# Where the softmax divides in the first sixteen pairs: on the output of a block of tokens, with the first two weight conversions done the older way

## The chip, the core and the metric

The kernel runs on one core of a Trainium2 chip. The metric is the device time of one execution in microseconds: 673.12 us, the median of three runs (672.76 to 674.39). Five things work side by side: TensorE (PE, matmuls, results into PSUM), VectorE (DVE), ScalarE (ACT), GpSimd (POOL, nearly unused here), and SyncE (SP), which issues the loads. Each has a queue of its own, worked off in the order in which the program wrote it; they meet through semaphores.

## What is computed

An attention with a window and four sink tokens, followed by two MLPs, on 2 x 768 tokens:

```
scores = q k^T / 8           2 batches, 8 heads, 768 tokens, head size 64
keep   = key < 4 (sinks)  or  0 <= query - key < 128
a      = exp(scores - max);   a = a / (sum(a) + 1e-9)
x      = a v                  -> 1536 tokens x 512
g      = max(h,0) + alpha*min(h,0),  h = x w_in      2048 wide
y      = g w_out
z      = (h2 - tanh(h2)) w_out2,     h2 = y w_in2
```

The weights come in as 64-bit floats and are turned into fp32 on the chip.

## The kernel before

Tokens are worked in twelve *blocks* `u` of 128, each in four *pairs* of heads: pair `n` = 4u + p, 48 in all. For a pair TensorE makes the scores of its two heads (`s_mm`, six matmuls, since queries and keys are split into a high and a low half), 288 columns wide: the block's own keys, the block's before, 32 sink keys. Block 0 has 128. VectorE adds the mask and takes the maximum (`s_max`, L279), ScalarE makes the exponentials with their row sums in the same instruction (`s_exp`, L288). VectorE adds 1e-9 to the sums and inverts them (`norm_sum`, L294, L296: "factors" below) and multiplies the two heads' rows by them (`norm`, L303). Only then does TensorE transpose the rows (`t_mm`, L319), alternating between the PSUM tiles `t` and `h`; ScalarE evicts them (`t_ev`, L326); TensorE multiplies them with the values (`pv`, L358, L359). From the third block of a batch on, the sink columns of two pairs are copied together (`sink_copy`, L309), transposed (`sink_mm`), evicted (`sink_ev`) and multiplied in (`pv`, L362). When a block's four pairs are there, its output in PSUM is split into a high half (`x_h`, ScalarE, L369) and a low half (`x_l`, VectorE, L374): the input of the first MLP.

The first 19 rounds `n` (S_LEAD) are attention alone, here called the lead. Round n makes the scores of pair n+1, maxima and exponentials of pair n, normalisation and transposes of pair n-1, outputs of pair n-2; a block's `x_h` stands at the end of the round after its last pair's transposes (n % 4 == 1), its `x_l` one round later. In between stand the splits of a key group for later pairs (`kq_hi` on ScalarE, L234, `kq_lo` on VectorE, L237; every other round) and two weight conversions, begun in rounds 8 and 12 and worked off one VectorE step a round. Of a conversion (`convert_scaled`) ScalarE does two steps (L73, L74), VectorE two (L76, L78), each 1024 columns wide. In round 14 the first weight is split for its matmuls (`split_w`, ScalarE, L215; `split_lo`, VectorE, L220).

After the lead the steps `g` of the MLPs begin (`h_mm`, `out_mm`), 96 in all, and the remaining pairs run among them, one a step (L678 to L801). The order is written out by hand: each engine gets its instructions in the order in which these lines call it, and the tiles' pools add the waits for a buffer to come free.

Of the kernel before, what the change touches and what calls it, by code (L numbers as in the profile page):

```python
# [9 lines left out]
F32 = mybir.dt.float32  # L10
# [5 lines left out]
AF = mybir.ActivationFunctionType  # L16
ALU = mybir.AluOpType
# [3 lines left out]


S_LEAD = 19
CONV0 = ((0, 8), (1, 12))
B, H, S, D = 2, 8, 768, 64
NB = S // 128
# [16 lines left out]
W_UP, W_DOWN = 2.0 ** -111, 2.0 ** -8  # L43
# [24 lines left out]
def convert_scaled(nc, pair, dst, seen):  # L68

    lw, hw = pair[:, :, 0], pair[:, :, 1]  # L70
    top = pair.bitcast(U16)[:, :, 1]
    di = dst.bitcast(I32)
    nc.scalar.activation(out=dst, in_=hw.bitcast(F32), func=AF.Abs, scale=W_UP, accum_out=seen)  # L73
    nc.scalar.activation(out=lw, in_=top, func=AF.Copy, scale=1.0 / 8192, bias=FLOOR)  # L74
    yield
    nc.vector.scalar_tensor_tensor(di, di, 3, lw, op0=ALU.logical_shift_left, op1=ALU.bitwise_or)  # L76
    yield
    nc.vector.scalar_tensor_tensor(di, hw, SIGN, di, op0=ALU.bitwise_and, op1=ALU.bitwise_or)  # L78
# [60 lines left out]
def fast_path(tc, qk, v, vsink, limits, w1i, w1o, alpha, w2i, w2o, out, outer):  # L139
    nc = tc.nc  # L140
    keep = outer.enter_context(tc.tile_pool(name="keep", bufs=1))
    bad_i = keep.tile([1, 1], I32, name="bad_i")
    with ExitStack() as ctx:
# [56 lines left out]
        def conv_w(m, f):  # L200
            raw = stage[m][f % 2]
            if m == 1 and f < 3:
                wf[m, f] = ap.tile([128, 1024], F32, name="wf", tag="wx" if f == 2 else "pq", bufs=1 if f == 2 else 2)
            else:
                wf[m, f] = wp.tile([128, 1024], F32, name="wf", tag="wf", bufs=NF)
            at = m * NF + f
            yield from convert_scaled(nc, raw.rearrange("p (n t) -> p n t", t=2), wf[m, f], seen[:, at:at + 1])

        whl = {}

        def split_w(m, c, f, part):
            src = wf[m, f][:, 512 * part:512 * part + 512]
            hi = wp.tile([128, 512], F32R, name=f"wh{part}", tag=f"wh{part}", bufs=2)
            lo = wp.tile([128, 512], F32R, name=f"wl{part}", tag=f"wl{part}", bufs=2)
            nc.scalar.activation(out=hi, in_=src, func=AF.Copy, scale=W_DOWN)  # L215
            whl[m, c, f, part] = (hi, lo)

        def split_lo(m, c, f, part):
            hi, lo = whl[m, c, f, part]
            nc.vector.scalar_tensor_tensor(lo, wf[m, f][:, 512 * part:512 * part + 512], W_DOWN, hi, op0=ALU.mult, op1=ALU.subtract)  # L220


        x_t, y_t = {}, {}
        pq, sums, ptb, pts, vps, sks, sps, tps = {}, {}, {}, {}, {}, {}, {}, {}
        initial = [True]
        rot = [0]

# [17 lines left out]
        def ps_tile(tags):  # L245
            rot[0] += 1
            tag = tags[rot[0] % len(tags)]
            return ps.tile([128, 512], F32, name="ps_" + tag, tag=tag, bufs=4 if tag == "o" else 1)
# [23 lines left out]
        def s_max(n, a):  # L272
            u, p, b, i, w = geom(n)
            G, hh = 2 * u + p // 2, 2 * (p % 2) + a
            if hh == 0:
                pq[G] = ap.tile([128, 4, 288], F32, name="pq", bufs=2)
                sums[G] = ap.tile([128, 4], F32, name="sums", bufs=2)
            mask = m_zero if i == 0 else m_one if i == 1 else m_even if i % 2 == 0 else m_odd
            nc.vector.tensor_tensor_reduce(  # L279
                out=pq[G][:, hh, 0:w], in0=sps.pop((n, a))[:, :w], in1=mask[:, 0:w], scale=-0.125, scalar=BIG,  # L280
                op0=ALU.add, op1=ALU.min, accum_out=nm[:, 2 * n + a:2 * n + a + 1],
            )

        def s_exp(n, a):
            u, p, b, i, w = geom(n)
            G, hh = 2 * u + p // 2, 2 * (p % 2) + a
            e = pq[G][:, hh, 0:w]
            nc.scalar.activation(out=e, in_=e, func=AF.Exp, scale=-1.0, bias=nm[:, 2 * n + a:2 * n + a + 1], accum_out=sums[G][:, hh:hh + 1])  # L288

        def norm_sum(n, part):  # L290
            u, p, b, i, w = geom(n)
            r = sums[2 * u + p // 2][:, 2 * (p % 2):2 * (p % 2) + 2]
            if part == 0:
                nc.vector.tensor_scalar(r, r, 1e-9, None, op0=ALU.add)  # L294
            else:
                nc.vector.reciprocal(r, r)  # L296

        def norm(n):
            u, p, b, i, w = geom(n)
            G, hh = 2 * u + p // 2, 2 * (p % 2)  # L300
            for a in range(2):
                e = pq[G][:, hh + a, 0:w]
                nc.vector.tensor_scalar(e, e, sums[G][:, hh + a:hh + a + 1], None, op0=ALU.mult)  # L303
        def sink_copy(n):
            u, p, b, i, w = geom(n)
            G = 2 * u + p // 2
# [4 lines left out]
        def t_mm(n):  # L311
            u, p, b, i, w = geom(n)
            G, hh = 2 * u + p // 2, 2 * (p % 2)
            tps[n] = t = ps_tile(["t", "h"] if initial[0] else ["t"])
            cur = 0 if i % 2 == 0 else 160
            for a in range(2):
                for e, c in ((0, 160 - cur), (1, cur)):
                    if i > 0 or e == 1:
                        nc.tensor.transpose(t[:, 256 * a + 128 * e:256 * a + 128 * e + 128], pq[G][:, hh + a, c:c + 128], ident)  # L319

        def t_ev(n):
            u, p, b, i, w = geom(n)
            ptb[n] = ap.tile([128, 2, 2, 128], F32, name="pt", bufs=2)
            e0 = 1 if i == 0 else 0
            tv = tps.pop(n).rearrange("p (a e c) -> p a e c", a=2, e=2)
            nc.scalar.activation(out=ptb[n][:, :, e0:, :], in_=tv[:, :, e0:, :], func=AF.Copy)  # L326
# [5 lines left out]
        def sink_mm(n, share):  # L332

            G = n // 2
            tag = ["o"] if initial[0] else ["s"]
            a = 1 if initial[0] else 0
            s = sps[share, a] if (share, a) in sps else ps_tile(tag)
            if share < NPAIR:
                sps[share, a] = s
            tps[n, 0] = s  # L340
            nc.tensor.transpose(s[:, 384:512], sks.pop(G).rearrange("p h c -> p (h c)"), ident)
# [22 lines left out]
        def x_h(n):  # L364
            u = n // 4
            c, off = divmod(u * 128, CH)
            if off == 0:
                x_t[c] = xp.tile([128, 2, 4, CH], F32R, name="x", tag="x")
            nc.scalar.activation(out=x_t[c][:, 0, :, off:off + 128], in_=vps[u], func=AF.Copy)  # L369

        def x_l(n):
            u = n // 4
            c, off = divmod(u * 128, CH)
            nc.vector.tensor_tensor(x_t[c][:, 1, :, off:off + 128], vps.pop(u), x_t[c][:, 0, :, off:off + 128], op=ALU.subtract)  # L374


        h_ps, gt, o_ps, mid, ob = {}, {}, {}, {}, {}
# [92 lines left out]
        nc.vector.memset(warm, 0.0)  # L470
        nc.vector.memset(shift, SQ_C)
        nc.vector.memset(limit, -POLY_T2)
        nc.vector.memset(m_one[:, 128:160], -BIG)
        nc.scalar.activation(out=warm, in_=warm, func=AF.Exp)
        load_qk(0)
# [79 lines left out]

        for n in range(S_LEAD):
            last = n == S_LEAD - 1
            a_loads(n)
            if n == 0:
                s_mm(0)  # L560
            if not last:
                s_mm(n + 1)
            if n >= 2:
                t_ev(n - 2)
            s_max(n, 0)
            s_max(n, 1)
            s_exp(n, 0)
            s_exp(n, 1)
            if n >= 2 and has_sinks(n - 2):
                sink_ev(n - 2)  # L570
            if n >= 1:
                norm_sum(n - 1, 0)
                norm_sum(n - 1, 1)
                norm(n - 1)
                sink_copy(n - 1)
                if not last:
                    t_mm(n - 1)
                    if has_sinks(n - 1):
                        sink_mm(n - 1, n + 1)
            if n >= 2 and not last:  # L580
                pv(n - 2)
            splits_hi(n)
            if n >= 5 and n % 4 == 1:
                x_h(n - 2)
            splits_lo(n)
            if n >= 5 and n % 4 == 2:
                x_l(n - 3)
            if n == 1:
                masks(0)
            if n == 4:  # L590
                masks(1)
            if n == 3:
                load_w(0, 1)
            for f, at in CONV0:
                if n == at:
                    conv_start(0, f)
                if at < n < at + 5:
                    conv_step(0, f)
                if n == at + 4:
                    load_w(0, f + 2)  # L600
                if n == at + 6 and f == 0:
                    split_w(0, 0, 0, 0)
                    split_lo(0, 0, 0, 0)
# [378 lines left out]
```

## Time and profile before

| | |
|---|---|
| median of 3 runs | 673.12 us |
| the profiled execution: its own time, its span | 672.06 us, 670.3 us |
| PE busy | 636.5 us, 95% |
| DVE busy | 526.3 us, 79% |
| ACT busy | 471.9 us, 70% |
| chain that ended last | PE 80%, DVE 8%, ACT 7% |

The page cuts the span into 40 slices of 16.8 us and gives busy shares in tenths (9 is 90% or more) and the clock granted to TensorE:

```profile
PE   4967999999999999999899999999999999999995
...
DVE  5887989899576665558877777889998888888873
ACT  4886988787566564557766767877877777777763
...
PEclk9997899999999999999999999999999999999999
```

A time line prints instructions in order of time: start, duration, engine, line, operation, tiles. Neighbours of one kind are merged (x4). A bracket says how long the engine had been idle before, and what ended the wait. VectorE and ScalarE overlap the end of one instruction with the start of the next, so a step (from start to start) is a little shorter than a duration.

### The profile page before, as it was taken

The page shows a single profiled execution, that of the slowest core. Times are in us where ns is not written, and L with a number is a line of the kernel's source. Part 1 is how long each engine was busy: PE and PEld are TensorE (multiplying, and loading weights), DVE is VectorE, ACT ScalarE, POOL GpSimd, SP SyncE. Part 2 cuts the span into 40 slices and gives each one's busy share as a digit, 9 for nine tenths or more (in the row PEclk, how much of TensorE's full clock was granted, in tenths as well). Part 3 has the DMA queues.
Part 4 walks back from the last instruction along what each step waited for, and adds up shares of the span by engine and source line. Part 5 has one row for each costly group of instructions (what it writes and reads, how often), then busy time and mean ns, then how long its engine had stood idle before and what let it go on. Part 6 is the DMA issues. An engine that isn't in the chain of part 4 may idle for free.

```text
span 670.3 us, 9201 instructions
## 1 busy us (share of the span) xinstructions
PE 636.5 (95%) x3194; PEld 501.2 (75%) x3194; DVE 526.3 (79%) x1098; ACT 471.9 (70%) x936; POOL 1.1 (0%) x8
## 2 busy tenths in 40 slices
PE   4967999999999999999899999999999999999995
PEld 2545677777777777777788887887888888888884
DVE  5887989899576665558877777889998888888873
ACT  4886988787566564557766767877877777777763
POOL 0000000000000000000000000000000000000000
PEclk9997899999999999999999999999999999999999
DMA  4752344453010000204343420100010000100001
GB/s 110 220 160 94 142 157 165 164 206 111 10 39 17 1 16 1 103 25 152 119 169 127 163 89 1 63 1 0 1 63 1 2 0 1 63 1 1 0 1 68
DMA packets 27032, 47.36 MB, mean 71 GB/s; under 512 B 3168, under 2 KB 15456, under 8 KB 26976
## 3 DMA queue, kind: packets, MB, share of 16 engines
q1 hardware_dynamic: 26976, 46.68, 20.3%
q8 instruction: 27, 0.44, 0.3%
q14 instruction: 29, 0.24, 0.1%
HBM read 43.53 MB, written 3.15 MB: 70 GB/s over the span
## 4 chain that ended last, share of the span: by engine, by line
PE 80%; DVE 8%; ACT 7%; issue 2%; SPq 1%; DMA 1%; ACTq 0%; DVEq 0%
PE ps_o L441 34%; PE ps_h L389 22%; PE ps_s L389 7%; PE ps_t L389 6%; PE ps_t L319 2%; PE ps_s L270 2%; PE ps_v L358 2%; PE ps_v L359 2%; PE ps_v L362 2%; ACT raw L74 1%; ACT wf L73 1%; PE ps_o L270 1%; DVE wf L78 1%; SPq L180 1%; DVE pq L279 1%
## 5 line engine op out<-in xcount | busy, mean ns | idle before, releaser
L220 DVE SCALAR_TENSOR_TENSOR wl<-wf,wh 128x512 fp32r<-128x512 f32 x192 | 123.6, 685 | 45.2 <-ACT wh L215 45.2
L389 PE MATMUL ps_h<-x,wh 128*128 128x512 f32 x384 | 124.5, 405 | 2.2 <-ACT t L396 1.9
L215 ACT ACTIVATE wh<-wf 128x512 fp32r<-128x512 f32 x192 | 111.0, 630 | 5.2 <-PE ps_o L441 5.2
L389 PEld LDWEIGHTS ps_h<-x,wh 128*128 128x128 f32 x384 | 68.7, 189 | 18.1 <-ACT t L396 3.1
L441 PE MATMUL ps_o<-gh,wh 128*128 128x512 f32 x192 | 76.6, 399 | 0.3 <-DVE y L452 0.3
L389 PE MATMUL ps_h<-x,wl 128*128 128x512 f32 x192 | 75.5, 393 | 0.0
L441 PE MATMUL ps_o<-wh,gh 128*128 128x512 f32 x192 | 74.8, 390 | 0.2 <-ACT gh L420 0.2
L441 PE MATMUL ps_o<-gh,wl 128*128 128x512 f32 x192 | 74.9, 390 | 0.0
L441 PE MATMUL ps_o<-gl,wh 128*128 128x512 f32 x192 | 74.8, 390 | 0.0
L441 PE MATMUL ps_o<-wh,gl 128*128 128x512 f32 x192 | 74.8, 390 | 0.0
L441 PE MATMUL ps_o<-wl,gh 128*128 128x512 f32 x192 | 74.7, 389 | 0.0
L288 ACT ACTIVATE pq<-pq,nm 128x288 f32<-128x288 f32 (+1 forms) x96 | 48.4, 506 | 28.6 <-DVE nm L279 28.2
L420 ACT ACTIVATE gh<-g 128x512 fp32r<-128x512 f32 x48 | 30.4, 633 | 36.4 <-DVE g L127 36.4
L76 DVE SCALAR_TENSOR_TENSOR wf<-wf,raw 128x1024 int32<-128x1024 int32 x32 | 39.1, 1222 | 18.7 <-ACT raw L74 18.6
L326 ACT ACTIVATE pt<-ps_t 128x512 f32<-128x512 f32 (+1 forms) x39 | 21.8, 560 | 35.5 <-PE ps_t L319 35.5
L441 PEld LDWEIGHTS ps_o<-gh,wh 128*128 128x128 f32 x192 | 36.1, 188 | 9.1 <-issue 1.4
L420 ACT ACTIVATE gh<-t 128x512 fp32r<-128x512 f32 x48 | 30.1, 627 | 18.1 <-DVE t L408 18.1
L389 PEld LDWEIGHTS ps_h<-x,wl 128*128 128x128 f32 x192 | 36.2, 188 | 8.0
L441 PEld LDWEIGHTS ps_o<-wh,gh 128*128 128x128 f32 x192 | 36.0, 188 | 8.1 <-ACT gh L420 0.6
L441 PEld LDWEIGHTS ps_o<-wh,gl 128*128 128x128 f32 x192 | 36.0, 188 | 7.9 <-DVE gl L425 0.4
L441 PEld LDWEIGHTS ps_o<-gh,wl 128*128 128x128 f32 x192 | 36.0, 188 | 7.8
L441 PEld LDWEIGHTS ps_o<-wl,gh 128*128 128x128 f32 x192 | 36.0, 188 | 7.5
(145 smaller groups left out, 1285.2 us busy)
## 6 DMA issues: line engine op xcount, KB each, us to landing
raw<-in_moe_w_in_dram SPq DMA_DIRECT2D x32, 512.0 KB, 3.3
raw<-in_moe_w_out_dram SPq DMA_DIRECT2D x32, 512.0 KB, 4.3
raw_qk<-in_qk_dram SPq DMA_DIRECT2D x96, 64.0 KB, 2.9
vt<-in_v_dram SPq DMA_DIRECT2D x12, 256.0 KB, 2.8
out_dram<-ob SPq DMA_DIRECT2D x2, 1024.0 KB, 4.2
out_dram<-ob SPq DMA_DIRECT2D x4, 256.0 KB, 3.4
vs<-in_vsink_dram SPq DMA_DIRECT2D x2, 256.0 KB, 3.6
ns_raw<-in_limits_dram SPq DMA_DIRECT2D x1, 2.0 KB, 2.6
```

What stands on the lines that cost most here:

```text
L76: nc.vector.scalar_tensor_tensor(di, di, 3, lw, op0=ALU.logical_shift_left, op1=ALU.bitwise_or)
L215: nc.scalar.activation(out=hi, in_=src, func=AF.Copy, scale=W_DOWN)
L220: nc.vector.scalar_tensor_tensor(lo, wf[m, f][:, 512 * part:512 * part + 512], W_DOWN, hi, op0=ALU.mult, op1=ALU.subtract)
L270: nc.tensor.matmul(sps[n, a][:, :w], lhsT=kq[l][h, p, at:at + 128], rhs=kq[r][h, p, K_EVEN:K_EVEN + w], start=e == 0, stop=e == 2)
L288: nc.scalar.activation(out=e, in_=e, func=AF.Exp, scale=-1.0, bias=nm[:, 2 * n + a:2 * n + a + 1], accum_out=sums[G][:, hh:hh + 1])
L319: nc.tensor.transpose(t[:, 256 * a + 128 * e:256 * a + 128 * e + 128], pq[G][:, hh + a, c:c + 128], ident)
L326: nc.scalar.activation(out=ptb[n][:, :, e0:, :], in_=tv[:, :, e0:, :], func=AF.Copy)
L358: nc.tensor.matmul(d, lhsT=vt[u - 1][:, h * D:(h + 1) * D], rhs=pt[:, a, 0, :], start=p == 0, stop=False)
L359: nc.tensor.matmul(d, lhsT=vt[u][:, h * D:(h + 1) * D], rhs=pt[:, a, 1, :], start=p == 0 and i == 0, stop=p == 3 and i < 2)
L389: nc.tensor.matmul(h_ps[f], lhsT=l[:, w], rhs=x[:, r, kk, :], start=kk == 0 and e == 0, stop=kk == 3 and e == 2)
L420: nc.scalar.activation(out=gh, in_=mid[f], func=AF.Copy)
L441: nc.tensor.matmul(o, lhsT=l, rhs=r, start=f == 0 and e == 0, stop=f == NF - 1 and e == 2)
```

## The change

For the pairs of the first four blocks (`u < LATE`) the rows are no longer normalised before they are transposed. Their sums lie in one tile of eight columns a block; after the fourth pair all eight are inverted at once. TensorE then spreads the factors: `late_mm` multiplies, head by head, a column of factors broadcast to 64 columns with the identity, so that a PSUM tile `ps_r` holds the factor of every token in every row of the block's output (eight matmuls). `late_copy` copies it to SBUF, `late_norm` multiplies the block's output in PSUM by it, and `x_h` and `x_l` read the product. `ps_r` lies where the second transpose tile lay, so in the lead the transposes have one tile in place of two. `x_h` moves from the end of round n % 4 == 1 into the next round, behind that round's exponentials and key split (in the last round it is issued earlier). Pairs 16 on are normalised as before.

The first two conversions use `convert_weights`: on ScalarE one step without a sum, on VectorE four. Their check against a limit goes away (`seen` is cleared at the start), and their weights need no scale.

```diff
+LATE = 4
...
@@ conv_w
+            if m == 0 and f < len(CONV0):
+                yield from convert_weights(nc, raw.rearrange("p (n t) -> p n t", t=2), wf[m, f])
+                return
             yield from convert_scaled(nc, raw.rearrange("p (n t) -> p n t", t=2), wf[m, f], seen[:, at:at + 1])
...
+        def down(m, f):
+            return 1.0 if m == 0 and f < len(CONV0) else W_DOWN
-            nc.scalar.activation(out=hi, in_=src, func=AF.Copy, scale=W_DOWN)
+            nc.scalar.activation(out=hi, in_=src, func=AF.Copy, scale=down(m, f))
...
@@ s_max, s_exp
-                sums[G] = ap.tile([128, 4], F32, name="sums", bufs=2)
+                if p == 0:
+                    sums[u] = ap.tile([128, 8], F32, name="sums", bufs=2)
...
@@ norm_sum
+            if u < LATE and p < 3:
+                return
+            r = sums[u] if u < LATE else sums[u][:, 2 * p:2 * p + 2]
...
@@ norm
+            if u < LATE:
+                return
...
+        def late_mm(n):
+            u = n // 4
+            rps[u] = ps.tile([128, 4, 128], F32, name="ps_r", tag="h", bufs=1)
+            for h in range(8):
+                a = 64 * (h % 2)
+                nc.tensor.matmul(rps[u][a:a + 64, h // 2, :], lhsT=sums[u][:, h:h + 1].to_broadcast([128, D]), rhs=ident, start=h < 2, stop=h >= 6)
+        def late_copy(n):
+            u = n // 4
+            xn[u] = gp.tile([128, 4, 128], F32, name="xn", tag="t", bufs=3)
+            nc.vector.tensor_copy(xn[u], rps.pop(u))
+        def late_norm(n):
+            u = n // 4
+            nc.vector.tensor_tensor(xn[u], vps.pop(u), xn[u], op=ALU.mult)
...
@@ t_mm
-            tps[n] = t = ps_tile(["t", "h"] if initial[0] else ["t"])
+            tps[n] = t = ps_tile(["t"])
...
@@ the lead, round n
             if n >= 2:
                 t_ev(n - 2)
+            if n >= 6 and n % 4 == 2:
+                late_norm(n - 3)
+                if last:
+                    x_h(n - 3)
             s_max(n, 0)
...
+            if n >= 5 and n % 4 == 1:
+                late_mm(n - 2)
             if n >= 2 and not last:
                 pv(n - 2)
+            if n >= 5 and n % 4 == 1:
+                late_copy(n - 2)
             splits_hi(n)
-            if n >= 5 and n % 4 == 1:
-                x_h(n - 2)
+            if n >= 6 and n % 4 == 2 and not last:
+                x_h(n - 3)
             splits_lo(n)
             if n >= 5 and n % 4 == 2:
                 x_l(n - 3)
```

`convert_weights`, which the general path had already, is this:

```python
    nc.scalar.activation(out=dst, in_=hw.bitcast(F32), func=AF.Abs)
    nc.vector.tensor_scalar(dst, dst, HW_LO, HW_HI, op0=ALU.max, op1=ALU.min)
    nc.vector.tensor_scalar(di, di, 5, 2, op0=ALU.logical_shift_left, op1=ALU.logical_shift_right)
    nc.vector.scalar_tensor_tensor(di, lw, 29, di, op0=ALU.logical_shift_right, op1=ALU.bitwise_or)
    nc.vector.scalar_tensor_tensor(di, hw, TOP2, di, op0=ALU.bitwise_and, op1=ALU.bitwise_or)
```

On VectorE, rounds 9 and 10. Before (from the key split of round 9 to the conversion step at the end of round 10; ISA is the masked maximum, `sk` the sink copy):

```order
L237 TENSOR_TENSOR kq_89<-raw_qk_257,kq_88 128x2x256
L76 SCALAR_TENSOR_TENSOR wf_423<-wf_423,raw1_90 128x1024
L279 ISA pq_471,nm_81<-ps_o_426,m_even_84 128x288
L279 ISA nm_81 128x1
L279 ISA pq_471,nm_81<-ps_o_427,m_even_84 128x288
L279 ISA nm_81 128x1
L294 TENSOR_SCALAR sums_404<-sums_404 128x2
L296 RECIPROCAL sums_404<-sums_404 128x2
L303 TENSOR_SCALAR pq_403<-pq_403,sums_404 128x288 x2
L309 COPY sk_481<-pq_403 128x128
L374 TENSOR_TENSOR x_318<-ps_v_351,x_318 128x4x128
L78 SCALAR_TENSOR_TENSOR wf_423<-raw1_90,wf_423 128x1024
```

And now (from the copy of the factors in round 9 on; `xn` is the SBUF tile of factors, later of the normalised output):

```order
L328 COPY xn_440<-ps_r_427 128x512
L244 TENSOR_TENSOR kq_89<-raw_qk_245,kq_88 128x2x256
L60 TENSOR_SCALAR wf_406<-wf_406 128x1024
L332 TENSOR_TENSOR xn_440<-ps_v_338,xn_440 128x512
L287 ISA pq_460,nm_81<-ps_o_408,m_even_84 128x288
L287 ISA nm_81 128x1
L287 ISA pq_460,nm_81<-ps_o_409,m_even_84 128x288
L287 ISA nm_81 128x1
L339 COPY sk_465<-pq_388 128x128
L405 TENSOR_TENSOR x_344<-xn_440,x_344 128x4x128
L62 TENSOR_SCALAR wf_406<-wf_406 128x1024
```

The normalisation and its factors are gone; a copy that reads TensorE's `ps_r` has come ahead of the key split, and a multiplication that reads `ps_v` ahead of the maxima of pair 10.

On ScalarE, rounds 8 to 10. Before (from the exponentials of pair 8; `pt` is the evicted transpose):

```order
L288 ACTIVATE pq_403,sums_404<-pq_403,nm_81 128x288 x2
L234 ACTIVATE kq_88<-raw_qk_257 128x2x256
L73 ACTIVATE wf_423,seen_83<-raw1_90 128x1024
L74 ACTIVATE raw1_90<-raw1_90 128x1024
L326 ACTIVATE pt_434<-ps_t_413 128x512
L288 ACTIVATE pq_403,sums_404<-pq_403,nm_81 128x288 x2
L369 ACTIVATE x_318<-ps_v_351 128x4x128
L326 ACTIVATE pt_469<-ps_h_444 128x512
L288 ACTIVATE pq_471,sums_472<-pq_471,nm_81 128x288 x2
L234 ACTIVATE kq_88<-raw_qk_321 128x2x256
```

And now:

```order
L296 ACTIVATE pq_388,sums_389<-pq_388,nm_81 128x288 x2
L241 ACTIVATE kq_88<-raw_qk_245 128x2x256
L58 ACTIVATE wf_406<-raw1_90 128x1024
L356 ACTIVATE pt_416<-ps_t_396 128x512
L296 ACTIVATE pq_388,sums_389<-pq_388,nm_81 128x288 x2
L356 ACTIVATE pt_457<-ps_t_422 128x512
L296 ACTIVATE pq_460,sums_389<-pq_460,nm_81 128x288 x2
L241 ACTIVATE kq_88<-raw_qk_312 128x2x256
L399 ACTIVATE x_344<-xn_440 128x4x128
L356 ACTIVATE pt_492<-ps_t_467 128x512
```

One conversion step is left of two, and `x` (the high halves of block 1) has moved from round 9, behind the exponentials of pair 9, to the end of round 10.

On TensorE, round 9, with the waits in brackets. Before (scores of pair 10, transposes of pair 8, the first of the outputs of pair 7):

```order
L270 MATMUL ps_o<-kq 128x288 x6
L319 MATMUL ps_h<-ident,pq 128x128 [waits DVE_49,PE_49]
L319 MATMUL ps_h<-ident,pq 128x128
L319 MATMUL ps_h<-ident,pq 128x128 [waits DVE_49]
L319 MATMUL ps_h<-ident,pq 128x128
L358 MATMUL ps_v<-pt,vt 64x128 [waits Activation_49]
L359 MATMUL ps_v<-pt,vt 64x128
```

And now:

```order
L277 MATMUL ps_o<-kq 128x288 [waits DVE_49] x2
L277 MATMUL ps_o<-kq 128x288 x4
L349 MATMUL ps_t<-ident,pq 128x128 [waits Activation_49]
L349 MATMUL ps_t<-ident,pq 128x128 x3
L323 MATMUL ps_r<-ident,sums 64x128 [waits DVE_49]
L323 MATMUL ps_r<-ident,sums 64x128 x7
L388 MATMUL ps_v<-pt,vt 64x128
```

The transposes wait for ScalarE (the exponentials, and the eviction that frees their only tile) where they waited for VectorE, and the eight factor matmuls stand between them and the outputs.

## Rows read from the trace of the kernel before

**Rows 1.** Table by stages: stage, length, each engine's busy us (instructions), granted clock, DMA.
```profile
26.00:48.00 22.00, 16.57 (x161) 11.92 (x161) 19.61 (x68) 19.28 (x53) 0.00 (x0) 1.00 0.51 155
48.00:58.00 10.00, 5.86 (x41) 4.25 (x37) 6.79 (x23) 5.46 (x15) 0.00 (x0) 0.66 0.45 151
...
66.00:160.00 94.00, 92.59 (x510) 68.84 (x509) 84.16 (x191) 77.71 (x165) 0.00 (x0) 0.98 0.49 168
```

**Rows 2.** Time line of TensorE, 22.5 to 30.6: start, us, engine line operation.
```profile
22.66 1.09 PE L270 MATMUL ps_o<-kq 64*128 64x288 f32 x6
...
24.72 0.70 PE L358 MATMUL ps_v<-pt,vt 128*64 128x128 f32 x4
...
25.78 0.90 PE L270 MATMUL ps_o<-kq 64*128 64x288 f32 x6
...
27.78 0.66 PE L270 MATMUL ps_o<-kq 64*128 64x288 f32 x6
28.38 0.64 PE L319 MATMUL ps_t<-ident,pq 128*128 128x128 f32 x4
28.96 0.45 PE L358 MATMUL ps_v<-pt,vt 128*64 128x128 f32 x4
...
29.55 0.67 PE L270 MATMUL ps_o<-kq 64*128 64x288 f32 x6
```

**Rows 3.** Time line of VectorE from 31.6.
```profile
32.80 0.45 DVE L279 CUSTOM_DVE_ANT_0 pq<-ps_o,m_even 128x288 f32<-128x288 f32 x1
...
33.55 0.17 DVE L294 TENSOR_SCALAR sums<-sums 128x2 f32<-128x2 f32 x1
...
33.95 0.65 DVE L303 TENSOR_SCALAR pq<-pq,sums 128x288 f32<-128x288 f32 x2
...
34.78 0.68 DVE L374 TENSOR_TENSOR x<-ps_v,x 128x512 fp32r<-128x512 f32 x1
35.38 1.22 DVE L78 SCALAR_TENSOR_TENSOR wf<-raw,wf 128x1024 int32<-128x1024 int32 x1
```

**Rows 4.** Time line of ScalarE from 27.3.
```profile
28.89 0.62 ACT L234 ACTIVATE kq<-raw_qk 128x512 fp32r<-128x512 f32 x1
29.41 1.12 ACT L73 ACTIVATE wf<-raw 128x1024 f32<-128x1024 f32 x1
...
30.53 1.09 ACT L74 ACTIVATE raw<-raw 128x1024 int32<-128x1024 uint16 x1
31.53 0.57 ACT L326 ACTIVATE pt<-ps_t 128x512 f32<-128x512 f32 x1
32.01 0.52 ACT L288 ACTIVATE pq<-pq,nm 128x288 f32<-128x288 f32 x1
...
33.04 0.57 ACT L369 ACTIVATE x<-ps_v 128x512 fp32r<-128x512 f32 x1
```

**Rows 5.** Time line of TensorE: scores of pairs 11, 15, 19, sinks, one gap.
```profile
32.75 0.66 PE L270 MATMUL ps_o<-kq 64*128 64x288 f32 x6
...
39.34 0.71 PE L362 MATMUL ps_v<-pts,vs 128*128 128x128 f32 x4
...
45.73 0.66 PE L270 MATMUL ps_o<-kq 64*128 64x288 f32 x6
...
52.43 0.45 PE L319 MATMUL ps_h<-ident,pq 128*128 128x128 f32 x1 [4.14 <-DVE pq L303]
...
65.74 0.40 PE L270 MATMUL ps_s<-kq 64*128 64x288 f32 x1 [1.74 <-ACT pts L345]
```

**Rows 6.** Time line of VectorE at 49 us; the bracket: idle before, and who ended it.
```profile
49.02 0.69 DVE L220 SCALAR_TENSOR_TENSOR wl<-wf,wh 128x512 fp32r<-128x512 f32 x1 [1.81 <-ACT wh L215]
```

**Rows 7.** Groups by line and shape, whole run: out<-in, count, busy us, mean ns, idle.
```profile
L303 DVE TENSOR_SCALAR pq<-pq,sums 128x288 f32<-128x288 f32 x80 | 26.0, 368 | 1.4
...
L455 DVE COPY ob<-ps_o 128x512 f32<-128x512 f32 x6 | 4.1, 690 | 2.5 <-PE ps_o L441 2.4
...
L303 DVE TENSOR_SCALAR pq<-pq,sums 128x128 f32<-128x128 f32 x16 | 3.9, 284 | 0.3
```

More of the change, by code (lines that the diff above doesn't have):

```diff
@@ L219, in split_lo @@
             hi, lo = whl[m, c, f, part]
-            nc.vector.scalar_tensor_tensor(lo, wf[m, f][:, 512 * part:512 * part + 512], W_DOWN, hi, op0=ALU.mult, op1=ALU.subtract)
+            nc.vector.scalar_tensor_tensor(lo, wf[m, f][:, 512 * part:512 * part + 512], down(m, f), hi, op0=ALU.mult, op1=ALU.subtract)
         x_t, y_t = {}, {}
-        pq, sums, ptb, pts, vps, sks, sps, tps = {}, {}, {}, {}, {}, {}, {}, {}
+        pq, sums, ptb, pts, vps, sks, sps, tps, rps, xn = {}, {}, {}, {}, {}, {}, {}, {}, {}, {}
         initial = [True]
@@ L287, in s_exp @@
             e = pq[G][:, hh, 0:w]
-            nc.scalar.activation(out=e, in_=e, func=AF.Exp, scale=-1.0, bias=nm[:, 2 * n + a:2 * n + a + 1], accum_out=sums[G][:, hh:hh + 1])
+            nc.scalar.activation(out=e, in_=e, func=AF.Exp, scale=-1.0, bias=nm[:, 2 * n + a:2 * n + a + 1], accum_out=sums[u][:, 2 * p + a:2 * p + a + 1])
         def norm_sum(n, part):
             u, p, b, i, w = geom(n)
-            r = sums[2 * u + p // 2][:, 2 * (p % 2):2 * (p % 2) + 2]
+            if u < LATE and p < 3:
+                return
+            r = sums[u] if u < LATE else sums[u][:, 2 * p:2 * p + 2]
             if part == 0:
@@ L300, in norm @@
             G, hh = 2 * u + p // 2, 2 * (p % 2)
+            if u < LATE:
+                return
             for a in range(2):
                 e = pq[G][:, hh + a, 0:w]
-                nc.vector.tensor_scalar(e, e, sums[G][:, hh + a:hh + a + 1], None, op0=ALU.mult)
+                nc.vector.tensor_scalar(e, e, sums[u][:, 2 * p + a:2 * p + a + 1], None, op0=ALU.mult)
+        def late_mm(n):
[11 more added lines that the diff above has]
+            nc.vector.tensor_tensor(xn[u], vps.pop(u), xn[u], op=ALU.mult)
         def sink_copy(n):
@@ L368, in x_h @@
                 x_t[c] = xp.tile([128, 2, 4, CH], F32R, name="x", tag="x")
-            nc.scalar.activation(out=x_t[c][:, 0, :, off:off + 128], in_=vps[u], func=AF.Copy)
+            nc.scalar.activation(out=x_t[c][:, 0, :, off:off + 128], in_=xn.get(u, vps.get(u)), func=AF.Copy)
         def x_l(n):
@@ L373, in x_l @@
             c, off = divmod(u * 128, CH)
-            nc.vector.tensor_tensor(x_t[c][:, 1, :, off:off + 128], vps.pop(u), x_t[c][:, 0, :, off:off + 128], op=ALU.subtract)
+            src = xn.pop(u) if u in xn else vps.pop(u)
+            nc.vector.tensor_tensor(x_t[c][:, 1, :, off:off + 128], src, x_t[c][:, 0, :, off:off + 128], op=ALU.subtract)
         h_ps, gt, o_ps, mid, ob = {}, {}, {}, {}, {}
@@ L472, in fast_path @@
         nc.vector.memset(limit, -POLY_T2)
+        nc.vector.memset(seen, 0.0)
         nc.vector.memset(m_one[:, 128:160], -BIG)
```

## The prediction, made before the changed kernel was run

> **What bounds the kernel now.** The page's slices show TensorE full from the fifth on. The table by stages says how full: from 66 to 160 us it is busy 92.6 of 94 us, but in the lead (26 to 48, 48 to 58) only 16.6 of 22 and 5.9 of 10 [rows 1]. So whatever moves the end of the lead moves the end of the kernel by as much; nothing behind it has slack to take a delay back. In the lead VectorE is the fullest engine, 19.6 of 22 us, ScalarE next with 19.3.
>
> The time line, read next, shows three regimes. Up to 25.8 us TensorE works without a gap and slowly: the outputs of a pair take 1.06 us (24.72 to 25.78), afterwards 0.59 (28.96 to 29.55) [rows 2]. Then queues that wait for one another bind the lead. Then, up to 52.43, TensorE stands for 4.14 us until a normalisation is done [rows 5]: VectorE had itself stood 1.81 us for a weight split of ScalarE [rows 6], with maxima and normalisation queued behind. The granted clock averages 0.66 in 48 to 58 [rows 1]: some 6.8 of these ten us at the lower level, 1.2 GHz, after that idle time.
>
> **Prices** (from one start to the next). VectorE: two masked maxima 0.75, a pair's factors 0.40, its normalisation 0.69, low halves of x 0.60 [rows 3]; low halves of a key group are the same 128x512 subtraction, 0.60; sink copy 0.15 (what is left between 33.95 and 34.78); a conversion step with two inputs 1.22 long, step 1.13. ScalarE: high halves of a key group 0.52, first conversion step 1.12 with its sum, second 1.00, eviction of transposes 0.48, two exponentials 1.03, high halves of x 0.57 until done [rows 4]; the single step of the older conversion has no sum, 1.05. TensorE: scores 0.60, transposes 0.58, outputs 0.59 [rows 2], sinks into the output 0.65 (0.71 long) [rows 5].
>
> Not in the trace: the eight factor matmuls. They have the shape of the output matmuls (64 columns of weights, 128 moving), four of which step 0.59 [rows 2], so 1.18, and 2.12 in the slow stretch. From below 0.59, if halves of the array hid each other wholly; from above eight times the 0.32 of a sink matmul, 2.6 [rows 5]. I take the equal shape. The copy of the factors out of PSUM: the copy of the results is 690 ns long [rows 7], as x's subtraction, so step 0.60; the multiplication likewise. The two added conversion steps of 1024 columns: TENSOR_SCALAR takes 284 ns for 128 columns and 368 for 288 [rows 7], 0.53 ns a column, so 0.76 long, step 0.70; the integer one is bounded above by the integer step with two inputs, 1.13. I take 0.70 for both, being the same operation; the other end costs 0.4 in each lap.
>
> The Trainium skill, "VectorE: DVE Perf Modes", section "Mode 2×_2P — use both read ports for one tensor", says that a single-source operation within SBUF gives two results a cycle even for fp32; of integers it makes no exception there, so by it 0.70 holds for both and the 0.4 falls away. No run shows the integer case yet.
>
> **The change, part by part.** It removes 32 normalisations and 12 pairs of factor operations from VectorE and two 1.00 us steps from ScalarE; it adds four copies, four multiplications and four wide steps on VectorE, and 32 matmuls. By loads a lap of four pairs loses 4 x 0.69 + 3 x 0.40 = 3.96 on VectorE and gains 2 x 0.60, and 2 x 0.70 with its conversion: 1.36 less. But each lap gets three meetings where one in-order queue waits for another:
>
> 1. The copy stands in VectorE's queue ahead of key halves, conversion, multiplication and the next maxima, and waits for the factor matmuls. These stand behind transposes, which, with one buffer in place of two, wait for the last eviction on ScalarE, behind the conversion there.
> 2. The multiplication waits for the outputs, which stand behind the factor matmuls. The maxima behind it have had their scores for long.
> 3. x's high halves now stand behind the exponentials (which wait for these maxima) and key halves on ScalarE, and x's low halves, with the conversion and the next maxima behind them, wait for that. Before, they did not wait (34.78) [rows 3].
>
> *Entry, to the scores of pair 11.* Early transposes no longer wait for factors and normalisation: about 0.5 earlier. The factor matmuls of block 0 then fall into the gapless slow stretch, +2.12; outputs of pair 3, which ended at 22.66 [rows 2], end at 24.25, the factor matmuls at 23.6. VectorE: copy, key halves, multiplication 25.45; maxima of pair 6 26.2. ScalarE: exponentials 26.95, key halves 27.47, x high 28.04. VectorE: x low 28.65, maxima of pair 7 29.4. ScalarE: exponentials 30.15, eviction 30.7, exponentials of pair 8 31.7, key halves 32.2, conversion 33.25, eviction of pair 7 33.8. TensorE: transposes of pair 8 34.45, factor matmuls of block 1 35.65, outputs 36.25: scores of pair 11 start at 36.25 against 32.75 [rows 5], +3.5.
>
> *Lap to pair 15.* VectorE: copy 36.3, key halves 36.9, conversion 37.6, multiplication 38.2, maxima of pair 10 38.95. ScalarE: exponentials 39.7, key halves 40.2, x high 40.78. VectorE: x low 41.4, conversion 42.1, maxima 42.85, key halves 43.45, conversion 44.6, maxima of pair 12 45.35, factors and sink copy 45.9, conversion 47.05. ScalarE meanwhile: exponentials of pair 12 46.1, key halves 46.6, conversion 47.65, eviction 48.2. TensorE: transposes of pair 12 48.85, factor matmuls of block 2 50.05, outputs 50.65, sinks 51.3: scores of pair 15 at 51.3 against 45.73 [rows 5], 15.05 in place of 12.98: +2.1.
>
> *Lap to pair 19.* The same chain, but here the kernel before has its 4.14 us gap and the doubled steps after it. Its weight split now follows x's high halves on ScalarE, so one wait serves both; and without so long a gap I leave the lower level out. Multiplication 52.6, maxima 53.35, exponentials 54.1, x high 55.18, split 55.73; x low, split's low halves, conversion 57.1, maxima of pair 15 57.85; key halves, conversion, maxima of pair 16 60.35; factors, sink copy, conversion 62.05, maxima of pair 17 62.8, normalisation of pair 16 (still the old way) 63.9. TensorE: transposes 64.5, factor matmuls, outputs, sinks 66.95. Multiplication 67.6, maxima of pair 18 68.35, exponentials 69.2, two steps of the third conversion 71.35, evictions 72.1: scores of pair 19 at 72.15 against 65.74 [rows 5], 20.85 in place of 20.01: +0.8.
>
> The sum is 3.5 + 2.1 + 0.8 = 6.4. The profiled execution took 672.06 (span 670.30), hence 678.5; it lay 1.06 under the median 673.12, so I predict 679.5.
>
> At nothing stand the clearing of 32 columns at the start (VectorE waits there for the first loads) and the other scale of two weights (an operand). Loads keep their places on SP.
>
> **Rivals.** *Faster: the loads decide.* Two laps with 1.36 less on the fullest engine give 2.7; the doubled steps, some 4 of the 5.9 us busy in 48 to 58, give 2 more: 673.1 - 4.7 = 668.4. For it speak VectorE's 19.6 of 22; against it, that the order is fixed. The gap before 52.43 shows the point: the maxima behind the waiting subtraction had their scores' matmuls issued from 45.73 on [rows 5, 6]. Chance 0.13.
>
> The Trainium skill, "PSUM — Partial Sum Buffer", section "Engine vs sequencer instructions", says that "ScalarE/VectorE/GpSimdE queues are strict FIFO"; by that rule this rival holds only if the meetings find their partners ready. The trace agrees with it at 49.02 [rows 6].
>
> *No change: new waits replace old ones.* TensorE idles 5.4 us in 26 to 48 and 4.1 in 48 to 58 [rows 1]. If the meetings fall into these, as I let them do in the last lap only, the laps lose nothing; the entry's extra 1.6, at the slow level, is half given back when the level rises, and the rest goes against the lighter VectorE: 673. Chance 0.10.
>
> *Slower still.* The factor matmuls at 2.6 in three laps add 4.2; or TensorE, idler in the lead, drops to the lower level again, 2 us as in 48 to 58 and more than once: 684 to 686. Chance 0.12.
>
> **How the numbers follow.** The forecast has 0.65 and its own range 676 to 683 (0.8 for the integer step above; matmuls, copy and level 2 to 3 either way). The range 672 to 685 adds most of "no change" and half of "slower still". 0.3%, about what can be told from no change, is 2.0 us: faster 0.14, same 0.10, slower 0.76.
>
> **What would show it.** Scores of pairs 11, 15 and 19 at about 36, 51 and 72 us. VectorE idle for 2 to 4 us before each copy out of the factors' PSUM tile and 1 to 2 before x's low halves, the latter released by ScalarE; factor matmuls at 1.18 a block; no gap of TensorE as long as 4 us before 66, and a granted clock near 1.00 in 48 to 58. I am wrong if the copies find their matmuls done, or if the scores of pair 19 start before 65.7.

## The result, and the profile after

The changed kernel takes 680.06 us (median of four runs, 679.18 to 681.3). Against runs of the kernel before on the same chip the ratio is 1.0100 (95% interval 1.0081 to 1.0119): slower by 1%, half a microsecond from the 679.5 predicted. The profiled execution took 680.0 us, span 678.1, 7.8 over the span of before.

The page's slices (tenths of busy time in 40 slices, and granted clock) differ most in the lead: in slices 2 to 4 VectorE falls from 8, 8, 7 to 4, 6, 7, and the clock is 8 in the second and third, where it was 9.

```profile
DVE  5467889799767655647886867898998887888883
...
PEclk9887899999999999999999999999999999999999
```

The table by stages answers to [rows 1] (stage, length, busy us of TensorE, weight loads, VectorE, ScalarE, GpSimd, granted clock, DMA); the last two lines are stretches in which the clock was low:

```profile
12.00:26.00 14.00, 11.85 (x79) 7.97 (x79) 8.15 (x37) 8.23 (x30) 0.00 (x0) 1.00 0.70 234
26.00:48.00 22.00, 17.57 (x130) 12.62 (x130) 13.18 (x43) 14.93 (x42) 0.00 (x0) 0.77 0.29 79
48.00:58.00 10.00, 6.73 (x70) 5.00 (x67) 5.96 (x17) 6.48 (x17) 0.00 (x0) 0.98 0.53 184
...
31.00:37.00 6.00, 6.00 (x40) 4.73 (x42) 0.96 (x6) 4.58 (x12) 0.00 (x0) 0.50 0.34 103
...
58.00:64.50 6.50, 5.95 (x34) 4.22 (x32) 6.26 (x22) 4.40 (x14) 0.00 (x0) 0.50 0.04 8
```

From 26 to 48 us VectorE is busy for 13.2 of 22 us, where it was 19.6, and ScalarE for 14.9 in place of 19.3. For VectorE that is mostly work taken away: normalisations and factors took 6.9 us in that stretch and take 0.7 now, while copy and multiplication add 1.4. For ScalarE it is the conversions: two of them took 4.9 us there, and now one takes 1.1, since the second starts at 48.02. The lighter engines got no further for it: pair 11 comes 4.8 us later. The waits of 12 to 74 us (engine, line, tile, releaser: total us, times, longest) name the partners:

```profile
ACT pq L296 <- DVE nm L287: 15.4, 8, 4.2
DVE xn L328 <- PE ps_r L323: 13.6, 4, 5.1
...
PE ps_t L349 <- ACT pt L356: 7.6, 5, 3.4
DVE x L405 <- ACT x L399: 5.3, 3, 1.9
```

VectorE's time line over the entry shows the first lap of these meetings, where [rows 3] has the maxima and normalisations of before:

```profile
23.65 0.69 DVE L328 COPY xn<-ps_r 128x512 f32<-128x512 f32 x1 [4.38 <-PE ps_r L323]
24.26 0.68 DVE L244 TENSOR_TENSOR kq<-raw_qk,kq 128x512 fp32r<-128x512 f32 x1
24.86 0.68 DVE L332 TENSOR_TENSOR xn<-ps_v,xn 128x512 f32<-128x512 f32 x1
25.46 0.45 DVE L287 CUSTOM_DVE_ANT_0 pq<-ps_o,m_one 128x288 f32<-128x288 f32 x1
...
28.16 0.69 DVE L405 TENSOR_TENSOR x<-xn,x 128x512 fp32r<-128x512 f32 x1 [1.87 <-ACT x L399]
28.77 0.45 DVE L287 CUSTOM_DVE_ANT_0 pq<-ps_o,m_one 128x288 f32<-128x288 f32 x1
...
37.14 0.69 DVE L328 COPY xn<-ps_r 128x512 f32<-128x512 f32 x1 [5.14 <-PE ps_r L323]
...
38.35 0.69 DVE L60 TENSOR_SCALAR wf<-wf 128x1024 f32<-128x1024 f32 x1
38.95 0.68 DVE L332 TENSOR_TENSOR xn<-ps_v,xn 128x512 f32<-128x512 f32 x1
```

VectorE stands 4.38 us before the copy, which waits for the factor matmuls. The maxima of pair 6 start at 25.46, behind copy, key halves and multiplication, though their scores were issued before these matmuls. ScalarE waits for the maxima, TensorE for ScalarE. TensorE's time line, against [rows 2, 5] (the trace has two records for each factor or output matmul, so eight factor matmuls are x16):

```profile
20.58 1.12 PE L349 MATMUL ps_t<-ident,pq 128*128 128x128 f32 x4
21.63 1.97 PE L323 MATMUL ps_r<-ident,sums 128*64 128x128 f32 x16
...
28.67 0.66 PE L349 MATMUL ps_t<-ident,pq 128*128 128x128 f32 x4 [1.66 <-ACT pt L356]
...
30.95 1.12 PE L349 MATMUL ps_t<-ident,pq 128*128 128x128 f32 x4 [0.42 <-ACT pt L356]
...
34.07 1.11 PE L349 MATMUL ps_t<-ident,pq 128*128 128x128 f32 x4
35.12 1.98 PE L323 MATMUL ps_r<-ident,sums 128*64 128x128 f32 x16
36.88 0.57 PE L388 MATMUL ps_v<-pt,vt 128*64 128x128 f32 x4
...
37.59 0.67 PE L277 MATMUL ps_o<-kq 64*128 64x288 f32 x6
...
40.58 0.48 PE L371 MATMUL ps_o<-ident,sk 128*128 128x128 f32 x1 [1.73 <-DVE sk L339]
...
50.26 1.09 PE L323 MATMUL ps_r<-ident,sums 128*64 128x128 f32 x16
51.18 0.44 PE L388 MATMUL ps_v<-pt,vt 128*64 128x128 f32 x4
...
52.41 0.66 PE L277 MATMUL ps_o<-kq 64*128 64x288 f32 x6
...
57.53 1.04 PE L349 MATMUL ps_t<-ident,pq 128*128 128x128 f32 x4 [1.19 <-ACT pt L356]
...
70.40 0.63 PE L349 MATMUL ps_t<-ident,pq 128*128 128x128 f32 x4 [2.39 <-DVE pq L315]
...
71.00 1.24 PE L420 MATMUL ps_h<-x,wh 128*128 128x512 f32 x2
...
73.88 0.61 PE L277 MATMUL ps_s<-kq 64*128 64x288 f32 x1
```

The scores of pairs 11, 15 and 19 start at 37.59, 52.41 and 73.88 us, in place of 32.75, 45.73 and 65.74 [rows 5]: 4.8 late after the entry, 6.7 after the next lap, 8.1 after the third. The span is 7.8 longer, so hardly anything behind the lead gave the delay back. The same eight factor matmuls step 1.76 us at 35.12 and 0.92 at 50.26: TensorE ran at its lower level, 1.2 GHz, from 31 to 37 us (granted clock 0.50; gaps of 1.66 and 0.42 us lay before), from 40.5 to 44 (0.51, behind a gap of 1.73) and from 57.5 to 64.5 (0.50 from 58 on, behind one of 1.19).

By form, the operations that no row of before showed (mean ns of one):

```profile
L328 DVE COPY xn<-ps_r 128x512 f32<-128x512 f32 x4 | 2.8, 691 | 13.6 <-PE ps_r L323 13.6
L332 DVE TENSOR_TENSOR xn<-ps_v,xn 128x512 f32<-128x512 f32 x4 | 2.7, 682 | 0.0
...
L60 DVE TENSOR_SCALAR wf<-wf 128x1024 f32<-128x1024 f32 x2 | 1.4, 685 | 0.0
L62 DVE TENSOR_SCALAR wf<-wf 128x1024 int32<-128x1024 int32 x2 | 1.4, 684 | 0.0
```

### The profile page after: what moved, and what is told of

Read it like the earlier page. It is cut to its first block, busy times and chain, and to the rows that moved or that the text cites. A ratio compares the mean times of both kernels' runs of the same rounds, so it can differ in the third digit from the quotient of the medians.

```text
span 678.1 us, 9278 instructions
## 1 busy us (share of the span) xinstructions
PE 645.1 (95%) x3258; PEld 508.6 (75%) x3258; DVE 520.4 (77%) x1055; ACT 470.0 (69%) x932; POOL 1.1 (0%) x8
## 4 chain that ended last, share of the span: by engine, by line
PE 77%; DVE 8%; ACT 7%; DMA 3%; issue 2%; SPq 1%; DVEq 0%; ACTq 0%
PE ps_o L472 33%; PE ps_h L420 21%; PE ps_s L420 6%; PE ps_t L420 6%; DMA raw<-in_moe_w_out_dram 3%; PE ps_t L349 2%; PE ps_s L277 2%; PE ps_v L388 1%; ACT pq L296 1%; PE ps_v L389 1%; ACT wf L74 1%; SPq L181 1%; DVE pq L287 1%; PE ps_v L392 1%; ACT raw L75 1%
## 5 line engine op out<-in xcount | busy, mean ns | idle before, releaser
L356 ACT ACTIVATE pt<-ps_t 128x512 f32<-128x512 f32 (+1 forms) x48 | 26.7, 556 | 38.3 <-PE ps_t L349 38.3
L77 DVE SCALAR_TENSOR_TENSOR wf<-wf,raw 128x1024 int32<-128x1024 int32 x30 | 36.7, 1222 | 16.8 <-ACT raw L75 16.8
L349 PE MATMUL ps_t<-ident,pq 128*128 128x128 f32 x176 | 32.3, 308 | 10.0 <-ACT pt L356 7.6
```

## Experiments

Each kernel ran in turn with the kernel before on one chip, and is judged by its ratio to it; the kernel before had medians of 673.5 to 674.8 us in these comparisons. My theory: the loss is the order of the new pieces in the engines' queues (three meetings), not their own time. Its rivals: the older conversions cost it; TensorE's additional work does; or TensorE's lower level after gaps.

### The two halves of the change

*Conversions alone*: the kernel before, with

```
+ if m == 0 and f < len(CONV0):
+     yield from convert_weights(...); return
```

> The kernel before with the second part of the change alone: the first two conversions the older way (one step on ScalarE, four on VectorE), division as before. Theory (the three meetings of queues carry the 7 us): this part is near neutral, each conversion taking 1.0 us from ScalarE and giving 1.4 to VectorE: 673, between 671.5 and 675. Rival (the four wide steps on VectorE, the fullest engine of the lead, carry the loss): 677 to 680.

Measured: 671.91 us, ratio 0.9959 (0.9946 to 0.9972). The older conversions are no part of the loss; they even gain a little. Where, the profiled execution doesn't show: it was the slowest of the eight (673.14), and its scores of pairs 11, 15 and 19 start at 32.79, 46.09 and 65.64, close to before.

*Division alone*: the changed kernel with `if False:` in place of that condition, and the scale of before.

> The changed kernel with the first two conversions as before (two steps on ScalarE with sum, two on VectorE): the division on the output alone. Theory of the meetings: 679 to 682, all of the loss, since ScalarE's longer conversion block stands in front of the eviction that meeting 1 waits for. Rival (conversions carry the loss): 673 to 675.

Measured: 684.83, ratio 1.0148 (1.0124 to 1.0172). More than expected: pair 19 starts at 78.49 us, 4.6 later than with the older conversions, which lack a second step of 1.00 us on ScalarE in each lap [rows 4]. In the entry the trace shows the step on the path: the eviction that frees the transposes' tile stands behind it (34.11 on ScalarE), the transposes of pair 8 wait 0.95 us for that eviction, and pair 11 starts at 38.60, 1.0 later. In the two laps, 2.3 and 1.3 us longer, TensorE's lower level has a share (granted clock 0.51 from 47 to 53.6 us and 0.52 from 61 to 70.9), and the step's own part there is argued, not shown. The halves add up, within the intervals: -0.41% and +1.48% against +1.00% together.

*No division at all in the first sixteen pairs*: neither factors nor normalisation, two tiles for the transposes.

> The changed kernel without any division in the first sixteen pairs: no factor matmuls, no copy, no multiplication, transposes with two tiles, x halves where the kernel before has them; so that part of the softmax is left out. It shows what taking the normalisations away could give at most. Theory: 667 to 671, since VectorE loses 4 us a lap and no queue waits anew. Rival (the laps are bound by something else, and the loads of VectorE do not count): 672 to 674.

Measured: 666.21, ratio 0.9866 (0.9839 to 0.9892), just below the range expected. Against the conversions alone the 32 normalisations and their factors are worth 0.93%, some 6 us. That is all that the change could win. It lost 2.34% against this version, some 16 us: the new pieces cost far more than the old ones.

### Which of the meetings

*All three loosened*, the same instructions in another order in the first three blocks:

```
- late_norm(n-3) ahead of the maxima (n % 4 == 2)
- late_mm(n-2); pv(n-2); late_copy(n-2)          (n % 4 == 1)
+ pv(n-2); late_mm(n-2)                          (n % 4 == 1)
+ late_copy(n-3); late_norm(n-3) behind maxima   (n % 4 == 2)
+ x_h one round later, x_l two rounds later
```

> The changed kernel, same instructions, other order for blocks 0 to 2: factor matmuls behind the outputs on TensorE, copy and multiplication behind the next pair's maxima on VectorE, x's high halves one round later and low halves two rounds later. The transposes keep one tile. Theory of the meetings: most of the loss goes, 673 to 676 (what is left: the factor matmuls at the slow level and the last block, whose order is kept). Rival (one transpose tile, or the factor matmuls' own time, sets the laps): 678 to 680.

Measured: 673.15, ratio 0.9983 (0.9966 to 1.0000). The same work without the loss: the order carries it.

*The first two*: as above, with `x_h` and `x_l` where the change has them.

> The changed kernel with two of the three meetings taken away in its first three blocks of tokens: the factor matmuls stand behind the outputs, and the copy and the multiplication one round later, behind that round's maxima; the conversion x high and x low stay in the round where the change has them. The reordering of all three was worth 7 us (680 to 673). If the first two meetings carry it, 673.5 to 676; if the third does (x low behind x high behind the exponentials and the key halves), 678 to 681, or more, since x high now waits for a later multiplication.

Measured: 673.33, ratio 0.9988 (0.9973 to 1.0004), the same. The third meeting is worth nothing that can be measured once the maxima are in time; VectorE still waits three times 0.70 us for ScalarE there.

*The copy and the multiplication alone*: both stand behind the next maxima; the factor matmuls stay ahead of the outputs.

```
- late_copy(n-2)                                 (n % 4 == 1)
- late_norm(n-3) ahead of the maxima             (n % 4 == 2)
+ late_copy(n-3); late_norm(n-3) behind maxima   (n % 4 == 2)
```

> The changed kernel with the copy of the factors moved one round later, in front of the multiplication and both behind that round's maxima; the factor matmuls stay ahead of the outputs. It parts the two meetings that the version with both moved (673.3) took away together. If the loss is VectorE's: the copy waits ahead of the maxima in its queue, 673 to 675. If it is TensorE's: the outputs behind the factor matmuls are late for the multiplication, 677 to 680.

Measured: 671.2, ratio 0.9962 (0.9942 to 0.9981), below both expectations. The whole loss hung on what VectorE had standing in front of its maxima. The waits of this version from 12 to 74 us:

```profile
ACT pq L296 <- DVE nm L287: 6.1, 6, 1.4
...
DVE xn L328 <- PE ps_r L323: 4.4, 4, 2.1
```

ScalarE's wait for maxima falls from 15.4 to 6.1 us, VectorE's for the factors from 13.6 to 4.4. VectorE's time line of this version:

```profile
20.62 0.46 DVE L287 CUSTOM_DVE_ANT_0 pq<-ps_o,m_one 128x288 f32<-128x288 f32 x1 [0.73 <-PE ps_o L277]
...
23.56 0.69 DVE L328 COPY xn<-ps_r 128x512 f32<-128x512 f32 x1 [2.10 <-PE ps_r L323]
...
33.52 0.69 DVE L328 COPY xn<-ps_r 128x512 f32<-128x512 f32 x1 [0.49 <-PE ps_r L323]
```

The copy starts at the same time, 23.56 against 23.65, since the factor matmuls end no earlier. But maxima ran at 20.62, while it would have waited, and the next lap's copy comes 3.6 us sooner. On TensorE the factor matmuls of block 1 step 0.92, and pairs 11 and 19 start at 33.89 and 64.64:

```profile
32.38 1.09 PE L323 MATMUL ps_r<-ident,sums 128*64 128x128 f32 x16
...
33.89 0.67 PE L277 MATMUL ps_o<-kq 64*128 64x288 f32 x6
...
64.64 0.40 PE L277 MATMUL ps_s<-kq 64*128 64x288 f32 x1
```

TensorE also keeps its upper level here (granted clock 1.00 from 26 to 57 us), so the gain includes what the level gives; the fill below prices that at 0.13% of the whole, not to be told from nothing. With the factor matmuls behind the outputs (the version before) the copy waited 9.3 us in all instead of 4.4, so that move was of no use.

*Two tiles for the transposes* in the changed kernel:

```
- tps[n] = ps_tile(["t"])                 ps_r: tag "h"
+ tps[n] = ps_tile(["t", "h"]) (the lead) ps_r: tag "v" if u % 2 else "s"
```

> The changed kernel with two PSUM tiles in turn for the transposed probabilities, as before; the spread factors lie in the bank of the outputs that is free at that time. The change left the transposes one tile, so that each set waits for ScalarE's eviction of the set before (waits of the transposes for it: 7.6 us from 12 to 74 us). If that is part of the way to the factor matmuls and so to the late maxima, 675 to 678; if ScalarE is late there only because it waits for the maxima itself, so that the second tile changes nothing, 679 to 681.

Measured: 679.92, ratio 1.0097 (1.0070 to 1.0123): no change. The transposes' wait for ScalarE's eviction is gone, but ScalarE still waits 13.9 us for maxima. By the median the one tile, which the prediction's first meeting named, was not what cost the time. The profiled execution is no typical one: at 677.73 it is the fastest of the four, 2 us under the median, with a higher clock than the others (0.991 against 0.987 and 0.988), and its pairs 11, 15 and 19 start at 33.67, 48.49 and 69.84, four us earlier than in the changed kernel. So a gain of some 2 us is not excluded.

### TensorE's time and level

*Factor matmuls twice*: `for h in [*range(8), *range(8)]`.

> The changed kernel with each block's eight factor matmuls issued twice, the second set writing the same values over the first. If they stand on the path of each block (the copy waits for them, and the maxima behind it), four times 0.92 us at the upper rate to 1.76 us at the lower one are added: 683.5 to 687. If they are hidden beside the other engines' waits, 679 to 681.

Measured: 683.79, ratio 1.0151 (1.0119 to 1.0183), 3.7 us more than the changed kernel, the lower end of what was expected; four times 0.92 is 3.7. In this order their time lies on the path, though not to the last tenth: pair 19 starts 2.9 us later (76.81). That the sum comes out so well is in part luck: in block 1 the doubled set ran at the upper level and took 1.80 us, about what the single one took at the lower, so pair 11 starts only 0.35 later. Order and own time are then not two causes: the matmuls' time counts because VectorE waits for them with its maxima behind the wait. Whether it still counts with the copy moved no run shows.

*Fill*: unread matmuls in four gaps.

```
+ if n in (7, 15):  10 x matmul(sps[n+1, 0][:, 288:384], ident, ident[:, 0:96])
  t_mm(n - 1)
+ if n in (10, 14):  8 x the same
```

> The changed kernel with 36 more matmuls of 96 columns, whose results nobody reads, in four gaps of TensorE: ten each ahead of the transposes in rounds 7 and 15, eight each ahead of the sinks in rounds 10 and 14. They add work to TensorE where it waits, and take away nothing. If the fall of TensorE to half its rate after these gaps costs time (matmuls at half rate from 30.95 to 37, 40.6 to 44 and 57.5 to 64 us in the changed kernel's trace), transposes, scores and factor matmuls there come back to the upper rate, and the time falls to 674 to 678. If the chain there is VectorE's and ScalarE's, or the fill is too short to hold the rate, 679.5 to 682.

Measured: 679.36, ratio 1.0087 (1.0056 to 1.0118): not to be told apart from the changed kernel, so the expectation of 674 to 678 fails. TensorE's time line says why:

```profile
30.95 0.66 PE L349 MATMUL ps_t<-ident,pq 128*128 128x128 f32 x4
...
34.52 1.09 PE L323 MATMUL ps_r<-ident,sums 128*64 128x128 f32 x16
...
36.03 0.66 PE L277 MATMUL ps_o<-kq 64*128 64x288 f32 x6
...
43.85 0.71 PE L392 MATMUL ps_v<-pts,vs 128*128 128x128 f32 x4 [1.31 <-ACT pts L375]
...
72.47 0.61 PE L277 MATMUL ps_s<-kq 64*128 64x288 f32 x1
```

The fill did hold the upper level: the transposes at 30.95 are 0.66 long in place of 1.12, the factor matmuls step 0.92 in place of 1.76, pair 11 starts at 36.03 in place of 37.59. Then, behind a gap that was not filled (1.31 at 43.85), the lower level came back (granted clock 0.59 from 45.8 to 50, 1.00 before and behind, to 69.5). Pair 19 came 1.4 us earlier, and of that only 0.2 is left in the span (677.9). The level is worth 1.6 us in the entry, and is not the loss: of the 8.1 us by which pair 19 is late, 6.7 remain.

### Candidates

*Three blocks* instead of four (`LATE = 3`; the fourth, whose pieces meet at the end of the lead, as before), in the order with all meetings loosened:

> The reordered kernel (673.2) with the division on the output in the first three blocks of tokens alone; the fourth block's eight divisions are made on the probabilities as in the kernel before. In the reordered kernel's trace the fourth block still has its three meetings, a copy 2.8 us late and ScalarE idle 3.5 us for the multiplication, which hold the exponentials of pair 18 until 60.7 us. If that is what is left of the loss, 669 to 671.5, at or below the kernel before with the older conversions alone (671.9); if the fourth block's divisions cost as much on VectorE as its meeting, 672.5 to 674.5.

Measured: 670.76, ratio 0.9961 (0.9944 to 0.9978), as expected.

*Spread further*: copy, multiplication, `x_h`, `x_l` each a round later than the last, two tiles where free.

> A candidate: the reordered version with three blocks (670.8), its pieces spread further: the copy at the end of the round after the factor matmuls, the multiplication in the third round, x high in the fourth, x low in the fifth, and a second PSUM tile for the transposes in the rounds in which the factors leave one free. If what is left of the loss is waits for the factors (3.5 us) and for the one tile (6.4 us), of which the version without any division shows at most 4.5 us to be had, 667.5 to 670; if these waits lie beside others, 670 to 672.

Measured: 670.83, ratio 0.9963 (0.9944 to 0.9981): no better.

*Copy moved, three blocks*:

> The version with the copy moved alone (671.2), and three blocks of tokens instead of four divided on the output: the fourth block, whose pieces meet at the end of the entry, divides its probabilities as before. In the fully reordered version the same step was worth 2.4 us (673.2 to 670.8). If the fourth block's meeting costs as much here, 668 to 669.5, the fastest that computes everything; if its eight divisions on VectorE cost what its meeting does, 670.5 to 672.

Measured: 672.12, ratio 0.9966 (0.9955 to 0.9978), the same as with four blocks (0.9962). That is just above the second of the ranges: here the fourth block's eight divisions cost what its meeting does.

The four best orders lie at 0.996 to 0.997 of the kernel before, a little faster than both kernels, and so does the kernel with the older conversions alone (0.9959). In its best order, then, the division on the output gains nothing over the division on the probabilities: it costs some 0.96% above the version without any, and the old way 0.93%.

## Why the prediction was right, and where it was off

The forecast went by the order, not by loads, and that was the decision that counted. The rival "loads decide" had 668.4 us. The loads did fall, but the lighter engines waited longer, and even with most of those waits gone (671.2) its time is not reached. That the total came within 0.6 us is in part luck, as the terms below show.

*The three meetings.* Two of the three are in the trace as waits: 13.6 us before the copies (4.4, 5.1, 2.3 and 1.8, where 2 to 4 were named), 5.3 before x's low halves, released by ScalarE as named. The second is not: the multiplication never waited for the outputs (L332, idle 0.0), which were done before its turn came; it only adds its 0.60 us ahead of the maxima. The predicted times of the entry came within about 0.1 us: multiplication done, hence maxima of pair 6, 25.45 (25.46); x low from 28.04 (28.16); maxima of pair 7 at 28.65 (28.77). There two errors nearly cancel: the first factor matmuls step 1.76 us, not 2.12, but began 0.15 later than forecast, and the copy starts 0.26 after the outputs took their place. The shares of the meetings were not told apart in the prediction. The runs did that: copy and multiplication ahead of the maxima are 1.4% (1.0100 to 0.9962), the place of x's halves nothing, the single tile nothing that can be measured. By the Trainium skill's "PSUM — Partial Sum Buffer", section "Engine vs sequencer instructions", the queues of ScalarE and VectorE are strict FIFO. The version with both behind the maxima agrees, with 9.3 us less of ScalarE's waiting for them.

*Entry, +3.5 predicted, +4.8 measured.* The mis-sized term is TensorE's level. I had the upper one from 25.8 on; it fell again (granted clock 0.50 from 31 to 37), after gaps of 1.66 and 0.42 us, and pair 8's transposes took 1.05 rather than 0.58, the factor matmuls of block 1 1.76 rather than 1.18. With the level held by the fill pair 11 starts at 36.03, against 36.25 predicted.

*Lap to pair 15, +2.1 predicted, +1.8 measured* (14.82 against 15.05). Factor matmuls at the upper level step 0.92, not 1.18, and a wide step takes 0.60 (38.35 to 38.95, copy and conversion alike), not 0.70. That the integer step takes as long as the fp32 one holds, 684 ns beside 685; both are shorter than the 0.76 us taken for them. The Trainium skill's "VectorE: DVE Perf Modes", "Mode 2×_2P — use both read ports for one tensor", gives two results a cycle to a single-source operation within SBUF and makes no exception for integers. The trace agrees: both steps take 0.68 us, the integer step with two inputs 1.22 [rows 3].

*Lap to pair 19, +0.8 predicted, +1.5 measured* (21.47 against 20.85). "I leave the lower level out" was wrong here, twice. The gaps were short, 1.19 us at 57.53, and the level fell all the same, to a granted clock of 0.50 from 58 to 64.5 us; with the level held there by the fill, the way from the scores of pair 15 to the factor matmuls of block 3 is 0.44 us shorter (12.94 in place of 13.38). And behind the gap of 2.39 before 70.40 it fell again (0.55 from 71 to 74): the MLP's first matmuls stand ahead of the scores of pair 19, which so start 0.54 us after ScalarE's last eviction was done (73.34), where before it was 0.06. The cheaper factor matmuls take 0.3 off. The clock in 48 to 58 came out as said, 0.98.

So the total, +6.4 against +7.8 in the span (+8.1 at pair 19), is short by three returns of the lower level, partly made up by cheaper matmuls and steps. A fourth, from 40.5 to 44, cost nothing that shows in its lap. The median of the runs lay only 0.06 over the profiled execution, where I had added 1.06 from the kernel before; that hid most of the difference, and is luck. The rival "slower still" named the level as what could be worse, with too large a price (684 to 686).

What stays open: where the older conversions gain their 0.4%, which the profiled executions don't show; and whether the second tile is worth up to 2 us.

## What to carry to other kernels

Before an operation is moved to a lighter engine or a smaller tensor, look at what it will stand in front of: an instruction that waits in an in-order queue delays everything behind it, and here the place of a copy and a multiplication of 0.6 us each was worth nine us. Put the reader of a slow partner behind the work that the next round needs, and let the partner start early. And price the work removed by leaving it out: some 6 us was all there was to win here, and the best order of the replacement costs as much.

## What the runs showed of the chip

TensorE's lower level (granted clock 0.50 or 0.51) came back after gaps of 1.66, 1.73 and 1.19 us between short bursts of matmuls, and 36 small matmuls in the gaps kept the upper one until one that was not filled. But the last gap alone doesn't tell: with the copy moved, gaps of 1.22 and 1.39 us left the transposes and scores behind them at the upper level, and with the factor matmuls doubled a gap of 1.81 did. Before the same transposes a gap of 1.22 us left them 0.66 long (copy moved, 31.79), and one of 1.21 made them 1.12 long (factor matmuls behind the outputs as well, 31.99). The granted clock of a stretch can hide a level: the table above has 1.00 for 12 to 26 us, in which transposes stepped 1.05 us at 20.58, where they step 0.58 later [rows 2]. Durations have to be read beside it. An integer operation of 1024 columns with one input takes the time of an fp32 one (684 and 685 ns). Eight fp32 matmuls with 64 columns of weights step 0.92 us at the upper level and 1.76 at the lower.
